# Seven half products for the gate and value products of two token groups, with a new order of the last third

## The chip, the cores and the metric

The kernel runs on one core of one Trainium2 chip. The metric is the device time of the whole program in microseconds, as the median of its runs. A core has a matrix engine (TensorE, PE in the profile), three engines for elementwise work (VectorE or DVE, ScalarE or ACT, GpSimd or POOL), and queues that start transfers (SyncE's above all, SP). Each engine works through its own list of instructions in order; semaphores hold an instruction until what it reads is written and what it overwrites is read. Matrix products end up in eight PSUM banks of 128 x 512 numbers (float32).

## The reference

Linear attention with exponential features over 8 batches, 8 heads and 576 tokens, then a feed-forward network over all 4608 tokens. Cut to what matters:

```python
def phi(x):                                   # 64 -> 128 -> 256 features
    proj = np.einsum('bhsd,df->bhsf', x, w_phi)
    proj = proj - np.max(np.abs(proj), axis=-1, keepdims=True)
    return np.concatenate([np.exp(proj), np.exp(-proj)], axis=-1)
q_p, k_p = (phi(q), phi(k))
kv = np.einsum('bhsf,bhsd->bhfd', k_p, v)
z = np.sum(k_p, axis=2)
num = np.einsum('bhsf,bhfd->bhsd', q_p, kv)
den = np.einsum('bhsf,bhf->bhs', q_p, z)[..., None] + 1e-06
x = (num / den).transpose(0, 2, 1, 3).reshape(4608, 512)
gate = np.maximum(x @ w_gate, 0.0)            # 512 -> 1536
val = x @ w_val                               # 512 -> 1536
out = gate * val @ w_out                      # 1536 -> 512
```

## The kernel before

**Groups.** The feed-forward network takes its tokens in nine groups of 512. Groups 0 to 7 are the first 512 tokens of each batch; group 8, the mixed group, holds the last 64 tokens of all eight batches. A group's x lies transposed in SBUF (`xTs`, four slots, for groups 0 to 7; `xTm` for the mixed group): 128 partitions, four blocks (`dc`) of 128 of the 512 columns. It gets there block by block: POOL normalises 128 tokens (`nx`, L947, into `xu`), and a transposing transfer from SP's queue (`xt`, L979) puts them into `xTs` or `xTm`.

**First product.** The 1536 columns of the gate and of the value weights (`wg`, `wv`) go in twelve chunks of 128. For each chunk `ffn_in` (L1081) issues four matmuls of 128 x 512 for the value product (`fv`) and four for the gate (`fg`), each into a bank. ACT (`va`, L1096) or DVE (`vb`, L1099) copies the value bank to SBUF (`val`), and DVE forms relu(gate) * value from the gate's bank and that copy into `h` (`ga`, L1102): 128 columns by 512 tokens in bf16. Of group 7 the `h` lies in two tiles of the ring `kp`, of the others in `h2` (16 slots, shown as `h`).

**Second product.** For groups 1 to 8 it is computed by seven half-sized products in place of eight. Per group, 24 half sums of `h` (four kinds for each of six pairs of chunks, 128 x 256 each; `half_sum`, L1223) are made on POOL (word `ps`) or on DVE (word `ds`; the 24 of the last part of groups 7 and 8), and differences of the weights `wo` once on POOL (`tw`, L1203). A half product (`fw`, L1247) is twelve matmuls of 128 x 256, six for each half of a bank. Copies and adds out of the banks (`ys`, `y2` on ACT, L1272 and L1275; `yw`, `yz`, `y1`, `y3`, `y4` on DVE, L1278) put the outputs together, and transfers (`ow` L1300 and others) write them out.

**Order.** A long string, `ORDER`, lists some 2,200 words such as `ga.7.4:1`: the name of a step, its arguments, the bank behind the colon, the ring slot behind the `@`. The program calls `do_<name>` for each word in turn, and each engine gets its instructions in that order. Nothing is moved afterwards. So the string alone sets what an engine does next, and an instruction that waits holds up everything behind it on its engine.

Of the kernel before, what the change touches and what calls it, by code (L numbers as in the profile page):

```python
# [16 lines left out]
ms.0 lf lm.0.0 ms.4@vr0 ms.6 id lk.0.2 lk.0.0 wq ms.3@vr1 if ms.5 zz.15:7 kf.0:0 ms.9 kf.1:1 zz.6:7  # L17
wd kh.0:0@kT0 sl k3.1.0:23 ke.0.1.0.0:2@kp0 w1:4 kg.1:1 kx.0.1.1:3@mk0 kx.0.1.0:2 wa:4 zz.2:7
k3.1.1:56 ke.0.1.3.0:6 lm.0.1 kx.0.1.2:5 zz.3:7 k0.2:0 lq.0.1 ke.0.1.3.1:6 k1.2:0@kT1 ke.0.1.0.1:2
zz.3:7 k0.0:1 ke.0.1.2.1:5 ke.0.1.1.1:3 k3.2.1:42 ke.0.1.2.0:5 kx.0.1.3:6 ms.2 lw.0.0 lw.0.1  # L20
k1.0:1@kT2 zz.5:7 k3.0.1:06 kk.0.1.0@ek0 k3.0.0:15 ke.0.1.1.0:3 ke.0.0.3.0:6@kp1 q0.1:3 lq.0.0
kx.0.2.3:2@mk1 kx.0.2.2:4 kk.0.1.1 ke.0.2.2.0:4@kp2 kx.0.0.0:1@mk2 kx.0.0.2:0 lv.0.1 ke.0.2.2.1:4
ke.0.0.1.1:5 kx.0.0.3:6 q1.1:3@qT0 ke.0.0.1.0:5 ke.0.0.3.1:6 lv.0.0 zz.6:7 q0.0:4 kx.0.0.1:5 wl.0.1
zz.4:7 k3.2.0:36 lv.0.2 ke.0.2.3.0:2 ke.0.0.2.1:0 ke.0.0.0.1:1 q1.0:4@qT1 ke.0.2.3.1:2 kx.0.2.1:6
zz.1:7 qb.1.1:5 zz.3:7 qb.0.1:4 kx.0.2.0:3 ke.0.0.0.0:1 zz.2:7 qb.0.0:2 qx.0.0.1:4 ke.0.0.2.0:0
zz.1:7 qb.1.0:1 qx.0.1.1:5 zz.7:7 qy.0.1:0 kp.0.0.0:2 ke.0.2.0.0:3 lk.1.3 kk.0.2.1@ek1 kp.0.0.1:2
kk.0.2.0 ke.0.2.1.1:6 vo.1@vs0 qx.0.1.0:1 qe.0.0.1.0:4@qp0 ke.0.2.0.1:3 qe.0.0.1.1:4 lq.1.2
qe.0.1.0.0:1@qp1 qe.0.1.0.1:1 vs.0.1.0 qz.0.1:0@my0 zz.4:7 qb.0.3:0 qx.0.0.0:2 zz.2:7 qy.0.0:3
vd.0.0.0:2@vs1 qz.0.0:3@my1 vs.0.1.1 qe.0.1.1.1:5 vp.0:2 qu.0.1@mz0 ke.0.2.1.0:6 qe.0.1.1.0:5 wl.0.0
vz.0:2 qb.0.2:4 zz.2:7 qb.1.3:3 zz.2:7 qb.1.2:1 vd.0.0.1:2 qu.0.0@mz1 vz.1:2 qe.0.1.3.0:3@qp2  # L30
vo.2@vs2 qw.0.0@cq0 qx.0.0.3:0 qx.0.0.2:4 qe.0.0.0.0:2 vs.0.2.1 zz.7:7 kv.0.0:6 qx.0.1.3:3 lw.1.1
vs.0.2.0 kc.0.0:6@kv0 kt.1.1@kT3 qe.0.0.0.1:2 kv.0.2:5 kv.0.1:6 qe.0.0.2.1:4@qp3 lm.1.1 kc.0.2:5
wl.1.1 kc.0.1:6 nu.0.0.0:2 nt.0.0.0:2@t0 zz.1:7 nu.0.0.2:5 qw.0.1 qx.0.1.2:1 qe.0.0.2.0:4
qe.0.1.3.1:3 nu.0.0.1:6 nv.0.0.0:2@u0 zz.2:7 nu.0.1.2:4 lv.1.2 nu.0.1.0:2 qe.0.1.2.1:1 nt.0.0.1:6@t1
lm.1.0 nt.0.0.2:5@t2 qy.0.2:3 nv.0.0.1:6 qe.0.0.3.0:0 nv.0.0.2:5 nt.0.1.0:2@t3 zz.2:7 nu.0.1.1:6
qy.0.3:5 nr.0.0@r0 qe.0.1.2.0:1 qz.0.2:3@my2 nv.0.1.0:2@u1 qz.0.3:5@my0 qu.0.2@mz2 zz.5:7
kr.1.1:3125 qe.0.0.3.1:0 nt.0.1.2:4@t0 nt.0.1.1:6@t1 qw.0.2 wl.1.0 nu.0.2.2:0 nx.0.0@xu0 nv.0.1.2:4
xp.0.0:7 nv.0.1.1:6 nt.0.2.2:0@t2 ke.1.1.3.1:5@kp3 nr.0.1@r1 nu.0.2.1:4 xa.0.0:7 nt.0.2.1:4@t3
nu.0.2.0:6 ke.1.1.0.1:3 nt.0.2.0:6@t0 qu.0.3@mz1 ke.1.1.0.0:3 pv.1.0:7 nv.0.2.1:4@u2 nv.0.2.2:0
nv.0.2.0:6 nu.0.3.1:4 qw.0.3 ke.1.1.1.0:1 nx.0.1@xu1 kx.1.1.0:3@mk3 xp.0.1:0 pa.1.0:7@val0  # L40
kx.1.1.3:5 pv.0.0:6 nr.0.2@r2 xa.0.1:0 nt.0.3.1:4@t1 nu.0.3.0:3 kx.1.1.1:1 nt.0.3.0:3@t3
ke.1.1.3.0:5 nu.0.3.2:7 kx.1.1.2:2 pa.0.0:6@val1 nt.0.3.2:7@t2 pv.1.1:0 nx.0.2@xu2 lw.1.0
nv.0.3.0:3@u0 xp.0.2:5 ke.1.1.1.1:1 pv.0.1:6 nv.0.3.2:7 pa.1.1:0@val2 pg.1.0:1 qt.1.1@qT2 ku.1@kT2
kk.1.1.0@ek2 ke.1.1.2.1:2 nv.0.3.1:4 pa.0.1:6@val3 lm.2.0 kt.1.0 nr.0.3@r0 nx.0.3@xu3 kk.1.1.1
qc.1.1:3076 ke.1.1.2.0:2 wl.0.2 pg.1.1:4 xa.0.2:5 pv.0.2:2 vo.1.1@vs3 qx.1.1.0:3 wl.1.2 pb.1.0:1
qe.1.1.1.0:0@qp4 qe.1.1.3.1:6@qp1 qe.1.1.0.0:3@qp0 qe.1.1.1.1:0 qx.1.1.2:7 pa.0.2:2@val0 xp.0.3:5
# [227 lines left out]
def kernel(  # L274
# [102 lines left out]
    def xT(g):  # L377
        return xT_mix if g == B else xT_all[:, g % 4]
# [985 lines left out]
```

## Time and profile before

| | |
|---|---|
| device time, median of 3 runs | 367.89 us (367.78 to 368.07) |
| span of the profiled execution | 365.2 us |
| TensorE (PE) busy | 356.6 us, 98% |
| DVE busy | 308.1 us, 84% |
| POOL busy | 275.8 us, 76% |
| ACT busy | 228.8 us, 63% |

The profile is of one execution; its own time is known by the span, first to last instruction, and the device time of the runs is 2.65 to 2.7 us longer. Busy shares are averages over stages with different limits. The page's forty slices show how the load moves (each digit is the busy share of 9.1 us in tenths):

```profile
PE   8999999999999999999999999999999999999993
DVE  5999999989999998989988989899676945448872
POOL 8765988999999999968997589946975793016600
```

TensorE is full from the second slice to the last but one. DVE and POOL are nearly full for the first two thirds and freer in the last third, where attention has ended and only the feed-forward network is left.

### The profile page before, as it was taken

To read this page: it belongs to the slowest core of one execution; us is meant where nothing else is said; L and a number is where in the kernel's file an instruction comes from. 1 tells how busy PE (TensorE), PEld (TensorE's weight loads), DVE (VectorE), ACT (ScalarE), POOL (GpSimd) and SP (SyncE) were. 2 spreads that over 40 slices of the span, in tenths; PEclk is the share of its full clock that TensorE was granted. 3 is DMA by queue.
4 is the path that set the end of the run, shared out by engine and by line. 5 is a ranking of instruction groups with operands and counts; after the bars stand their busy time and mean duration, and the time that the engine had idled before them with its cause. 6 is when DMAs were issued, how large, how long until landed. Compare 5 with 4: busy or idle time off the path is not lost.

```text
span 365.2 us, 10031 instructions
## 1 busy us (share of the span) xinstructions
PE 356.6 (98%) x3900; PEld 224.4 (61%) x3900; DVE 308.1 (84%) x723; ACT 228.8 (63%) x550; POOL 275.8 (76%) x337
## 2 busy tenths in 40 slices
PE   8999999999999999999999999999999999999993
PEld 6579865445575647755676456755457765545682
DVE  5999999989999998989988989899676945448872
ACT  4999996986698768695975278748854221121200
POOL 8765988999999999968997589946975793016600
PEclk9999999999999999999999999999999999999998
DMA  8999999983746893298219660397000320203016
GB/s 128 254 205 206 176 196 143 181 132 53 131 96 131 103 156 71 58 149 109 61 63 126 130 130 0 61 177 137 0 16 2 131 45 0 72 3 115 2 33 197
DMA packets 90768, 38.14 MB, mean 104 GB/s; under 512 B 64226, under 2 KB 86370, under 8 KB 90722
## 3 DMA queue, kind: packets, MB, share of 16 engines
q0 software_dynamic: 33504, 15.03, 32.5%
q1 hardware_dynamic: 56754, 21.83, 27.7%
q10 hardware_dynamic: 464, 0.66, 0.8%
q8 instruction: 30, 0.49, 0.6%
q14 instruction: 16, 0.13, 0.1%
HBM read 37.81 MB, written 9.44 MB: 129 GB/s over the span
## 4 chain that ended last, share of the span: by engine, by line
PE 81%; DVE 9%; POOL 4%; issue 2%; DMA 1%; ACT 1%; SPq 0%; DVEq 0%; POOLq 0%
PE bank L1081 42%; PE bank L1247 18%; PE bank L781 4%; PE bank L1110 4%; PE bank L904 3%; PE bank L1142 2%; PE bank L841 2%; PE bank L579 2%; POOL vs L1223 2%; DVE t L925 1%; DVE h L1102 1%; DVE u L935 1%; DMA w64f<-in_w_phi_dram 1%; ACT kp L675 1%; PE bank L442 1%
## 5 line engine op out<-in xcount | busy, mean ns | idle before, releaser
L675 ACT ACTIVATE kp<-bank 128x384 bf16<-128x384 f32 x192 | 84.1, 513 | 12.8 <-PE bank L579 6.0
L1081 PE MATMUL bank<-xTs,wv 128*128 128x512 bf16 x352 | 87.3, 379 | 0.0
L1096 ACT CAST val<-bank 128x512 bf16<-128x512 f32 x81 | 47.4, 592 | 62.8 <-PE bank L1081 55.7
L1081 PE MATMUL bank<-xTs,wg 128*128 128x512 bf16 x352 | 86.4, 379 | 0.0
L1102 DVE SCALAR_TENSOR_TENSOR h<-bank,val 128x512 bf16<-128x512 f32 x88 | 59.0, 681 | 22.1 <-PE bank L1081 15.0
L856 ACT ACTIVATE qp<-bank 128x512 bf16<-128x512 f32 x128 | 69.8, 619 | 5.3 <-PE bank L841 2.6
L1081 PEld LDWEIGHTS <-wg 128*128 128x128 bf16 x400 | 37.2, 98 | 41.0 <-issue 2.2
L1081 PEld LDWEIGHTS <-wv 128*128 128x128 bf16 x400 | 37.1, 98 | 38.0 <-DMA xTs<-xu 0.4
L732 POOL TENSOR_TENSOR vs<-vn,ek 128x780 bf16<-128x780 f32 (+2 forms) x40 | 53.9, 1364 | 1.2 <-ACT ek L692 0.7
L947 POOL TENSOR_TENSOR xu<-u,r 128x512 bf16<-128x512 f32 x36 | 37.3, 1044 | 16.8 <-DVE r L943 16.6
L683 DVE TENSOR_REDUCE mk<-bank 128x3 f32<-128x384 f32 x96 | 49.1, 542 | 1.0 <-ACT kp L675 0.9
L1247 PEld LDWEIGHTS <-h 128*128 128x128 bf16 x420 | 39.9, 98 | 9.5 <-issue 2.4
L1223 POOL TENSOR_TENSOR vs<-h 128x256 bf16<-128x256 bf16 x42 | 28.0, 670 | 21.4 <-DVE h L1102 14.4
L864 DVE TRANSPOSE_TENSOR_REDUCE maxq<-bank 128x16 f32<-128x512 f32 x56 | 37.1, 691 | 0.4 <-PE bank L841 0.2
L935 DVE TENSOR_TENSOR u<-bank,t 128x195 f32<-128x195 f32 (+1 forms) x108 | 32.7, 327 | 0.7
L925 DVE TENSOR_TENSOR t<-bank,cq 128x195 f32<-128x195 f32 (+1 forms) x96 | 29.4, 325 | 2.0 <-PE bank L904 1.7
L1247 PE MATMUL bank<-wo,h 128*128 128x256 bf16 x252 | 31.0, 273 | 0.0
L904 PEld LDWEIGHTS <-qp 128*128 128x128 bf16 x512 | 23.2, 98 | 10.8 <-issue 1.2
L1223 POOL TENSOR_TENSOR vs<-vs,h 128x256 bf16<-128x256 bf16 x42 | 27.9, 673 | 1.0 <-PE bank L1247 0.2
L904 PE MATMUL bank<-kv,qp 128*128 128x65 bf16 x512 | 26.1, 193 | 0.4 <-DVE u L935 0.2
L1223 POOL TENSOR_TENSOR h<-h 128x256 bf16<-128x256 bf16 x36 | 23.7, 670 | 0.3
L1223 POOL TENSOR_TENSOR h<-h,vs 128x256 bf16<-128x256 bf16 x36 | 23.7, 671 | 0.0
(134 smaller groups left out, 577.3 us busy)
## 6 DMA issues: line engine op xcount, KB each, us to landing
vn<-in_v_dram SPq DMA_DIRECT2D x24, 256.0 KB, 5.5
out_dram<-xTs SPq DMA_DIRECT2D x17, 256.0 KB, 2.4
kn<-in_k_dram POOLq DMA_DIRECT2D x7, 512.0 KB, 8.6
qn<-in_q_dram POOLq DMA_DIRECT2D x7, 512.0 KB, 8.0
out_dram<-obp SPq DMA_DIRECT2D x14, 256.0 KB, 2.4
wv<-in_moe_w_val_dram POOLq DMA_DIRECT2D x3, 512.0 KB, 8.9
wg<-in_moe_w_gate_dram POOLq DMA_DIRECT2D x3, 512.0 KB, 9.3
wo<-in_moe_w_out_dram POOLq DMA_DIRECT2D x3, 512.0 KB, 8.2
```

The costliest lines, as they stand in the source:

```text
L675: nc.scalar.activation(kp_of(3 * b + j)[:, i, s].rearrange("p n f -> p (n f)"), bank[bk[0]][:, 0 : 3 * F], AF.Exp, scale=(1.0, -1.0)[s],)
L683: nc.vector.tensor_reduce(mk_of(3 * b + j)[:, :, i], bank[bk[0]][:, 0 : 3 * F].rearrange("p (n f) -> p n f", f=F), axis=AX.X, op=ALU.max, ...
L732: nc.gpsimd.tensor_tensor(vs_of(3 * b + j)[:, s, 0:n].rearrange("p n i e -> p (n i) e")[:, :, 0:e], src[:, lo:hi].rearrange("p h i e -> p ...
L856: nc.scalar.activation(qp_of(4 * b + i)[:, s, 4 * hq : 4 * hq + 4].rearrange("p h m -> p (h m)"), bank[bk[0]], AF.Exp, scale=(1.0, -1.0)[s],)
L864: nc.vector.tensor_reduce((maxq0[:, i] if b == 0 else maxq)[:, :, i, 4 * hq : 4 * hq + 4].rearrange("p t h -> p h t"), bank[bk[0]].rearran ...
L904: nc.tensor.matmul(bank[bk[0]][:, E * n : E * (n + 1)], lhsT=qp_of(4 * b + i)[:, s, h, :], rhs=kv_of(b)[:, h, s, 0:E],)
L947: eng.tensor_tensor(xu_of(n).rearrange("p (h d) -> p h d", d=D), u_of(n)[:, :, 0:D], r_of(n).to_broadcast([P, H, D]), op=ALU.mult,)
L1081: nc.tensor.matmul(bank[bk[0]], lhsT=w[:, dc, P * f : P * f + P], rhs=xT(g)[:, dc, :], start=(dc == 0), stop=(dc == NDC - 1),)
L1096: nc.scalar.copy(val_of(NFC * g + f), bank[bk[0]])
L1102: nc.vector.scalar_tensor_tensor(h2_of(g, f), bank[bk[0]], 0.0, val_of(NFC * g + f), op0=ALU.max, op1=ALU.mult)
L1223: eng.tensor_tensor(sum_of(g, n, j), a, b, op=op)
L1247: nc.tensor.matmul(bank[bk[0]][:, col : col + HN], lhsT=x[:, P * u : P * (u + 1)], rhs=w, start=(n in (1, 5, 6) and u == us[0] and j == 0) ...
```

## The change

The first product of two groups, 8 and 7, is now computed together, with seven half products in place of eight. As a block product, the rows are the tokens of group 8 (x1, x2: the two halves of the 512 columns of x) and of group 7 (x3, x4), and the columns are the gate and the value weights, each in an upper and a lower half. With S1 = x3 + x4, S2 = S1 - x1, S3 = x1 - x3, S4 = x2 - S2 for the tokens and T1 = wv_lo - wg_lo, T2 = wv_hi - T1, T3 = wv_hi - wv_lo, T4 = wg_hi - T2 for the weights, seven products of two matmuls each are made per chunk: P1 = x1 wg_lo, P2 = x2 wg_hi, P3 = S4 wv_hi, P4 = x4 T4, P5 = S1 T1, P6 = S2 T2, P7 = S3 T3. The gate of group 8 is P1 + P2; its value P1 + P6 + P3 + P5; the value of group 7 is P1 + P6 + P7 + P5, its gate P1 + P6 + P7 + P4.

- The word `fi.p.f.n` is product n of chunk f (two matmuls; p = 0 is the only pair). It takes the place of `fv` and `fg` of groups 7 and 8.
- P1 is needed twice more: ACT copies its bank to another bank (`ia`), TensorE adds P6 there, and ACT copies that bank to a third (`ib`). P5 is copied to SBUF by ACT (`iq`, into a float32 tile of the ring `u`).
- DVE forms the two values as bank plus that copy (`iv`, two for each chunk). They replace the copies `va` and `vb` of groups 7 and 8. The gate of group 7 is made in the bank that its value was read from, so P4 follows `iv`.
- POOL makes the token sums (`xs`, eight operations of 128 x 512, L1169) and the weight sums (`wt`, 24 of 128 x 512, L1142). T3 overwrites the lower half of `wv`.
- The 24 half sums that DVE made (`ds`) are now made on POOL (`ps`). One copy of the keys' product moves from ACT to DVE.
- The `h` of group 7 lies in one `kp` tile, one `qp` tile and two slots of `h2`.
- `ORDER` is new for its last quarter (from about 241 us in the trace on); ahead of that only banks and ring slots have other numbers.

```diff
     def h2_of(g, f):
         i = NFC * g + f
-        if g == B - 1:
-            t = kp_of(("h", g, f // 6)).rearrange("p i s n f -> p (i s n f)")
-            return t[:, SF * (f % 6) : SF * (f % 6 + 1)]
+        if g == B - 1 and f < 6:
+            t = kp_of(("h", g)).rearrange("p i s n f -> p (i s n f)")
+            return t[:, SF * f : SF * (f + 1)]
+        if g == B - 1 and f < 10:
+            t = qp_of(("h", g)).rearrange("p s h m -> p (s h m)")
+            return t[:, SF * (f - 6) : SF * (f - 5)]
...
+    PAIRS = ((8, 7),)
...
+    def weight_sum(eng, n, dc, third):
+        cols = slice(SF * third, SF * (third + 1))
+        at = lambda t, d: t[:, d, cols]
+        a, b = {
+            1: lambda: (at(wv_sb, dc), at(wg_sb, dc)),
+            2: lambda: (at(wv_sb, 2 + dc), at(w_sum(1), dc)),
+            3: lambda: (at(wv_sb, 2 + dc), at(wv_sb, dc)),
+            4: lambda: (at(wg_sb, 2 + dc), at(w_sum(2), dc)),
+        }[n]()
+        eng.tensor_tensor(at(w_sum(n), dc), a, b, op=ALU.subtract)
+
+    def do_wt(bk, n, dc, third):
+        weight_sum(nc.gpsimd, n, dc, third)
...
+    def token_sum(eng, p, n, dc):
+        a, b, op = {
+            1: lambda: (x_part(p, 3), x_part(p, 4), ALU.add),
+            2: lambda: (x_sum(p, 1), x_part(p, 1), ALU.subtract),
+            3: lambda: (x_part(p, 1), x_part(p, 3), ALU.subtract),
+            4: lambda: (x_part(p, 2), x_sum(p, 2), ALU.subtract),
+        }[n]()
+        eng.tensor_tensor(x_sum(p, n)[:, dc], a[:, dc], b[:, dc], op=op)
+
+    def do_xs(bk, p, n, dc):
+        token_sum(nc.gpsimd, p, n, dc)
+
+    def do_fi(bk, p, f, n):
...
+        for dc in range(2):
+            nc.tensor.matmul(
+                bank[bk[0]],
+                lhsT=w[:, dc, P * f : P * f + P],
+                rhs=x[:, dc, :],
+                start=(n in (1, 5) and dc == 0),
+                stop=(dc == 1),
+                skip_group_check=(n not in (1, 5)),
+            )
+
+    def do_ia(bk, p, f):
+        nc.scalar.copy(bank[bk[1]], bank[bk[0]])
+
+    def do_ib(bk, p, f):
+        nc.scalar.copy(bank[bk[1]], bank[bk[0]])
+
+    def do_iq(bk, p, f):
+        nc.scalar.copy(q_evicted(p, f), bank[bk[0]])
...
+    def do_iv(bk, p, f, u):
+        nc.vector.tensor_tensor(
+            val_of(NFC * PAIRS[p][u] + f), bank[bk[0]], q_evicted(p, f), op=ALU.add
+        )
```

Two lines of the new `ORDER`, from its middle:

```python
iv.0.3.0:2@val2 iv.0.3.1:0@val1 fi.0.0.4:6 fi.0.6.1:5 fi.0.3.2:7 fi.0.6.5:2 wt.2.0.2 ia.0.6:51
fi.0.9.5:0 iq.0.8:6@u1 fi.0.6.4:1 iv.0.4.0:4@val1 iv.0.7.1:3@val0 wt.2.1.2 ps.6.4.4 wt.3.0.2
```

The instructions of POOL in the stretch in which group 7's x is finished. Rows give the line, the operation, out<-in and the shape; `xu` is a normalised block, `qT` and `qr` hold token sums, `vn`, `kp` and `wv` weight sums, and `vs` and `h` half sums. Before:

```order
L947 TENSOR_TENSOR xu_135<-u_127,r_131 128x512
L1223 TENSOR_TENSOR h_152<-h_152,vs_98 128x256 x2
L1223 TENSOR_TENSOR vs_97<-h_152 128x256
L1223 TENSOR_TENSOR h_152<-h_152,vs_98 128x256
L1223 TENSOR_TENSOR vs_100<-vs_97,h_152 128x256
L1223 TENSOR_TENSOR vs_97<-h_152 128x256
```

After the same normalisation in the new program:

```order
L960 TENSOR_TENSOR xu_133<-u_127,r_131 128x512
L1337 TENSOR_TENSOR vs_98<-h_152 128x256
L1169 TENSOR_TENSOR qT_108<-xTs 128x512 x2
L1169 TENSOR_TENSOR qT_107<-qT_108,xTm 128x512
L1337 TENSOR_TENSOR h_152<-h_152 128x256
L1337 TENSOR_TENSOR vs_97<-vs_98,h_152 128x256
L1337 TENSOR_TENSOR h_152<-h_152 128x256
L1169 TENSOR_TENSOR qT_107<-qT_108,xTm 128x512
```

Token sums, which read the transposed x in `xTs` and `xTm`, stand between the half sums of group 6; the weight sums follow behind them, among half sums.

The end of POOL's list, with the half sums of groups 8 (`h`, `vs`) and 7 (`kp`, `qp`, `vs`), before:

```order
L1223 TENSOR_TENSOR vs_101<-kp_82,kp_81 128x256 x2
L1223 TENSOR_TENSOR vs_99<-vs_101,kp_82 128x256
L1223 TENSOR_TENSOR vs_100<-vs_97,h_152 128x256 x3
L1223 TENSOR_TENSOR vs_101<-kp_82,kp_81 128x256 x3
L1223 TENSOR_TENSOR vs_99<-vs_101,kp_82 128x256 x5
```

And of the new program:

```order
L1337 TENSOR_TENSOR vs_101<-kp_83,qp_112 128x256
L1337 TENSOR_TENSOR vs_98<-vs_101,kp_83 128x256 x3
L1337 TENSOR_TENSOR h_152<-h_152,vs_99 128x256 x2
L1337 TENSOR_TENSOR vs_98<-vs_101,kp_83 128x256 x2
L1337 TENSOR_TENSOR h_152<-h_152,vs_99 128x256
L1337 TENSOR_TENSOR kp_83<-kp_83 128x256
L1337 TENSOR_TENSOR h_152<-h_152,vs_99 128x256 x3
L1337 TENSOR_TENSOR kp_83<-kp_83 128x256 x3
L1337 TENSOR_TENSOR h_152<-h_152,vs_98 128x256
L1337 TENSOR_TENSOR qp_112<-qp_112,vs_98 128x256 x4
L1337 TENSOR_TENSOR h_152<-h_152,vs_98 128x256
```

The sums that overwrite `h`, `kp` and `qp` (third and fourth kind) now close POOL's list. Before they stood near the end of DVE's, between the adds of the output:

```order
L1223 TENSOR_TENSOR kp_81<-kp_81,vs_99 128x256
L1223 TENSOR_TENSOR kp_82<-kp_82 128x256
L1278 TENSOR_TENSOR xTs<-bank_65,xTs 128x2x256
L1223 TENSOR_TENSOR kp_81<-kp_81,vs_99 128x256 x2
L1223 TENSOR_TENSOR h_152<-h_152,vs_100 128x256
L1278 TENSOR_TENSOR obp<-bank_66,obp 128x2x256
L1223 TENSOR_TENSOR h_152<-h_152,vs_100 128x256
L1278 TENSOR_TENSOR obp<-bank_64,obp 128x2x256
```

The same place of DVE's list in the new program, where only the adds are left behind the last product with relu:

```order
L1118 SCALAR_TENSOR_TENSOR qp_112<-bank_67,val_141 128x512
L1392 TENSOR_TENSOR xTm<-bank_68,obp 128x2x256
L1392 TENSOR_TENSOR obp<-bank_68,obp 128x2x256 x2
L1392 TENSOR_TENSOR obp<-bank_64,obp 128x2x256
L1392 TENSOR_TENSOR xTs<-bank_69,xTs 128x2x256
L1392 TENSOR_TENSOR xTm<-bank_64,xTm 128x2x256
L1392 TENSOR_TENSOR xTs<-bank_69,xTs 128x2x256
```

More of the change, by code (lines that the diff above doesn't have):

```diff
@@ L23 @@
[L23 to L46, printed above, removed]
```

533 lines of the change are left out of this document (304 added, 229 removed).

## The prediction

> **What bounds the kernel now.** Read the page's busy times first, then the chain of waits, then the windows of the last 85 us (columns: stretch, length, then busy time and count of PE, PEld, DVE, ACT, POOL, the granted clock, DMA share, GB/s).
>
> ```profile
> span 365.2 us, 10031 instructions
> PE 356.6 (98%) x3900; PEld 224.4 (61%) x3900; DVE 308.1 (84%) x723; ACT 228.8 (63%) x550; POOL 275.8 (76%) x337
> PE 81%; DVE 9%; POOL 4%; issue 2%; DMA 1%; ACT 1%; SPq 0%; DVEq 0%; POOLq 0%
> 280.00:300.00 20.00, 20.00 (x253) 14.29 (x251) 13.17 (x44) 5.17 (x11) 17.66 (x27) 1.00 0.28 80
> 300.00:320.00 20.00, 20.00 (x112) 10.75 (x110) 10.31 (x16) 3.01 (x6) 4.68 (x7) 1.00 0.11 33
> 320.00:340.00 20.00, 20.00 (x100) 9.70 (x99) 13.12 (x23) 4.26 (x8) 8.61 (x13) 1.00 0.15 54
> 340.00:350.00 10.00, 10.00 (x84) 8.03 (x82) 8.30 (x16) 2.48 (x5) 5.29 (x8) 1.00 0.01 2
> ```
>
> TensorE is busy in every microsecond of this stretch at full clock, and the chain runs on it for 81% of the span. POOL is the freest engine there: 13.3 us of 40 between 300 and 340. The timeline says how TensorE is paid.
>
> ```profile
> 302.71 1.03 PE L1081 MATMUL bank<-xTm,wg 128*128 128x512 bf16 x4
> 303.57 1.03 PE L1081 MATMUL bank<-xTm,wv 128*128 128x512 bf16 x4
> 342.03 1.47 PE L1247 MATMUL bank<-wo,h 128*128 128x256 bf16 x12
> 357.75 1.47 PE L1247 MATMUL bank<-wo,kp 128*128 128x256 bf16 x12
> 359.26 0.42 DVE L1278 TENSOR_TENSOR xTs<-bank,xTs 128x256 f32<-128x256 f32 x1 [0.23 <-PE bank L1247]
> ```
>
> Four matmuls of 128x512 start 0.86 us after the four before them: 0.2155 each. The thirteen groups of twelve half-wide matmuls from 342.03 end with the last at 357.75 + 1.31 = 359.06 (1.31 is (357.75 - 342.03)/12): 0.109 per matmul, no gap. The last add starts 0.20 later, and the final output's transfer follows it. From TensorE's end to the span's end are 365.24 - 359.06 = 6.18 us, and the median of the runs, 367.89, lies 2.65 above the span. So **time = TensorE's end + 8.83**, if what follows the last matmul stays; the after's order ends in the same way (last half product, one add, one output transfer).
>
> **The change, part by part.** *Removed from TensorE.* Twelve chunks x two products x eight matmuls become twelve x seven x two: 192 - 168 = 24 fewer, and 24 x 0.2155 = 5.17 us. With no new stall TensorE ends at 353.89.
>
> *Added to POOL.* Eight token sums and 24 weight sums (512 wide, two bf16 inputs), and 24 half sums of groups 7 and 8 that DVE made.
>
> ```profile
> 240.98 2.04 POOL L947 TENSOR_TENSOR xu<-u,r 128x512 bf16<-128x512 f32 x2 [3.42 <-DVE r L943]
> 282.26 0.67 POOL L1223 TENSOR_TENSOR vs<-h 128x256 bf16<-128x256 bf16 x1
> 282.89 0.67 POOL L1223 TENSOR_TENSOR vs<-vs,h 128x256 bf16<-128x256 bf16 x1
> 284.15 0.67 POOL L1223 TENSOR_TENSOR vs<-h 128x256 bf16<-128x256 bf16 x1
> 284.89 1.30 POOL L1223 TENSOR_TENSOR vs<-vs,h 128x256 bf16<-128x256 bf16 x2
> L947 POOL TENSOR_TENSOR xu<-u,r 128x512 bf16<-128x512 f32 x36 | 37.3, 1044 | 16.8 <-DVE r L943 16.6
> L732 POOL TENSOR_TENSOR vs<-vn,ek 128x780 bf16<-128x780 f32 x24 | 35.5, 1497 | 0.5 <-ACT ek L692 0.4
> L732 POOL TENSOR_TENSOR vs<-vn,ek 128x520 bf16<-128x520 f32 x12 | 12.6, 1061 | 0.3 <-ACT ek L692 0.3
> L760 POOL TENSOR_TENSOR vr<-vm,ek 64x520 bf16<-64x520 f32 x14 | 14.8, 1059 | 1.3 <-ACT ek L692 0.7
> L1203 POOL TENSOR_TENSOR kp<-wo 128x768 bf16<-128x768 bf16 x4 | 6.6, 1647 | 0.0
> ```
>
> Starts lie some 0.04 us before the end of the one ahead, so an operation holds POOL for its duration less 0.04: a half sum 0.63 (282.26 to 282.89). A 512-wide sum of two bf16 inputs is not in the trace. By the rows of 256 (0.63) and 768 (1.60) it is the midpoint, 1.11; by the 512-wide normalisation it is 1.00. I take **1.11**, since those rows are of the same form. The normalisations at 240.98 stand at the same place of both orders, and nothing ahead of them changes but names of banks and buffers. From there to its end POOL has, in the new order, 94 half sums, 32 of the new sums, 10 normalisations, 4 value products of 780, 2 of 520 and 2 of the 64-row kind: 94 x 0.628 + 32 x 1.11 + 10 x 1.00 + 4 x 1.45 + 2 x 1.01 + 2 x 1.02 = 114.4 us (before: 114.4 - 24 x 0.628 - 35.5 = 63.8). **With no wait at all POOL ends at 355.4**, later than the 353.89 of TensorE. POOL takes the bound over.
>
> *The end.* The last sum is the sixth fourth-kind sum of group 7. Behind it TensorE has one half-wide matmul of the first half and the six of the second, 0.11 + 0.66: end at 356.2.
>
> *POOL's waits.* Each goes straight to the end.
>
> ```profile
> 242.05 3.42 SPq L979 DMA_TRANSPOSE xTs<-xu  x1
> 287.96 1.22 SPq L979 DMA_TRANSPOSE xTm<-xu  x1
> xTm<-xu SPq DMA_TRANSPOSE x4, 3.2
> 324.16 0.67 POOL L1223 TENSOR_TENSOR vs<-kp,kp 128x256 bf16<-128x256 bf16 x1 [15.48 <-DVE kp L1102]
> ```
>
> Three of the eight sums that make group 8's inputs (second kind, and what follows) wait for the transposed last block of the mixed group; its normalisation ends at about 285.7 by my sum over POOL's order, and 3.2 us to landing (row of issues) make 288.9, where POOL stands ready at 288.5: 0.4 us. Where a sum reads what the one ahead wrote, starts lie 0.74 apart (284.15 to 284.89), 0.11 more; about eight such pairs stand in the new order: 0.9. Sum 1.3. Below, it could be 0; above, the row at 324.16 shows POOL waiting 15.48 us for group 7's h in one go, so the upper end is open; what speaks for a small one is that POOL, at its new load, comes later to every sum of groups 6 to 8 than before, so that the h it reads has had longer to be ready. I take **1.3: TensorE ends at 357.5 to 357.6, 1.5 us earlier than before, time 366.4**.
>
> *Removed from DVE.* 24 half sums and seven value copies go; 24 adds of a bank to a buffer come, and one copy of the keys' products.
>
> ```profile
> L1223 DVE TENSOR_TENSOR kp<-kp,vs 128x256 bf16<-128x256 bf16 x6 | 1.6, 281 | 0.0
> 344.23 3.37 POOL L1223 TENSOR_TENSOR vs<-vs,kp 128x256 bf16<-128x256 bf16 x5
> 344.34 0.75 DVE L1223 TENSOR_TENSOR kp<-kp 128x256 bf16<-128x256 bf16 x1
> 353.32 0.28 DVE L1223 TENSOR_TENSOR kp<-kp,vs 128x256 bf16<-128x256 bf16 x1
> L1278 DVE TENSOR_TENSOR obp<-bank,obp 128x512 f32<-128x512 f32 x21 | 14.2, 681 | 4.3 <-PE bank L1247 4.3
> L1102 DVE SCALAR_TENSOR_TENSOR h<-bank,val 128x512 bf16<-128x512 f32 x88 | 59.0, 681 | 22.1 <-PE bank L1081 15.0 <-ACT val L1096 5.1 <-PE bank L1247 1.1
> ```
>
> The new adds read a bank and a buffer, as the last two rows do (0.681): 24 x 0.68 = 16.3 us. The half sums cost DVE 0.28 each alone and 0.75 beside POOL's, 6.7 to 18 us in all. So DVE's load rises by at most some 10 us, in 70 (280 to 350) in which the windows leave it 70 - 13.17 - 10.31 - 13.12 - 8.30 = 25 idle: nothing on the path by its load alone. In before's tail POOL made five sums at 3.37/5 = 0.675 while DVE summed from buffers, and at 0.63 where DVE did not: I use 0.628 for the tail's 22, since no DVE sum with two buffer inputs is left there. The Trainium skill, "SBUF — State Buffer", section "Who interferes with whom", states that a DVE instruction with two SBUF inputs contends with a GpSimd instruction that reads SBUF, and that one with at most one SBUF input doesn't; the 0.675 and 0.75 agree with it. Without that rule the 22 sums would take 22 x 0.047 = 1.0 us more and the time would be 367.4.
>
> *Evictions.* 24 copies of values (17 on ACT, 7 on DVE) go; 36 copies on ACT come, 24 of them from bank to bank.
>
> ```profile
> L703 ACT ACTIVATE bank<-mk 128x12 f32<-128x12 f32 x2 | 0.4, 180 | 0.0
> L1096 ACT CAST val<-bank 128x512 bf16<-128x512 f32 x25 | 14.3, 587 | 41.0 <-PE bank L1081 36.6 <-DVE h L1102 4.2
> ```
>
> No 512-wide copy into a bank is in the trace; the value copies (0.587) are its nearest row, the 12-wide write (0.18) bounds it below, and the adds of 0.681 above. I take 0.59. A chunk then needs 3 x 0.59 = 1.8 us of ACT and 4 x 0.68 = 2.7 us of DVE (two adds, two products with relu) beside 14 x 0.2155 = 3.02 us of TensorE: each fits. But a product that adds to a bank now waits for the copy into it, and the order leaves such waits no slack: at six places, walking the new order with these prices gives -0.2 to +0.1 us. Up to 1.2 us of TensorE's stalls there are free, since POOL reaches the tail's sums at 341.6 and group 7's last h is ready at 340.4 without stalls.
>
> **The rivals.**
>
> *(a) The forecast*, POOL the bound at the end: from waits 0 to 2.0, TensorE's end 356.2 to 358.2, time 365.0 to 367.0. For it: 114.4 us in 118.
>
> *(b) POOL is cheaper, TensorE stays the bound.* With 1.00 per 512-wide sum POOL saves 32 x 0.11 = 3.5 and ends at 351.9 + waits; then eviction stalls of 0 to 1.5 on 353.89 set the end: 362.7 to 364.3. Against it: the bf16 rows.
>
> *(c) All is given back*, by 1.5 us more of POOL's waits for h, as TensorE's stalls behind the bank copies exceed the free 1.2 us: end 359.1, time 367.9. Work that is saved only moves the wait; this is also how it looks if the matmuls saved come back as stalls.
>
> *(d) Slower, by the token sums' wait for the transposes.* If the transposed blocks of group 7 and the mixed group come later, as with the one at 242.05 that took 3.42 us to issue where the one at 287.96 took 1.22, POOL stands still at its fullest place, all weight sums slip, and with them the matmuls that read them: 1.2 for the wait on group 7's block and 1.5 for the mixed group's, 2.7 in all, end 360.3, time 369.1. It decides as soon as POOL's waits from 240.98 on sum to over 1.3 + 1.5 + 0.7 = 3.5 us. For it: even before, POOL stands idle for 2.3 us of 280 to 300, where it is fullest.
>
> That the change doesn't remove the matmuls is excluded: the program has 7729 TensorE instructions where 7777 stood.
>
> **How the numbers follow.** (a) 0.50, (b) 0.12, (c) 0.18, (d) 0.20. Faster by over 0.2% (0.74 us, about what a measurement of this kernel can tell from no change) means under 367.15: (a) and (b), 0.62. Within 0.2%: (c), 0.18. Slower: (d), 0.20. The likeliest is (a): **366.4**. The range leaves out the lower two thirds of (b) and the tail of (d) beyond 369.6, some 0.15: from 363.9 to 369.6; the own range of (a) is 365.0 to 367.0.
>
> **What would show it.** TensorE: 3876 matmul records, fewer by 24; its last matmul ends at about 357.6, with gaps of together 3 to 4 us after 300, most of them ended by POOL in the last 15 us. POOL: busy over 19 of each 20 us from 280 on; token and weight sums of 1.15 (1.11 + 0.04); the last half sum ends at about 356.7. ACT: bank copies of 0.59. Wrong would be: 512-wide sums near 1.04 (then b); gaps of TensorE ended by ACT or DVE that sum to over 3 us (c); a gap of POOL of over 1 us ahead of a token sum, ended by a DMA (d).

## The result, and the profile after

| | before | after |
|---|---|---|
| device time, median | 367.98 us (367.78 to 368.26, 4 runs) | 362.22 us (361.98 to 362.58, 4 runs) |
| ratio, 95% interval | | 0.9847 (0.9833 to 0.9861) |
| span of the profiled execution | 365.2 us | 360.8 us |
| last matmul, nominal end | 359.06 | 357.06 |
| last matmul to the span's end | 6.2 | 3.7 |

The change makes the kernel 5.8 us faster, below the predicted range. First the page of the changed kernel (span, busy times, chain of waits), then its windows (same columns as before).

```profile
span 360.8 us, 10067 instructions
PE 354.0 (98%) x3876; PEld 222.5 (62%) x3876; DVE 309.8 (86%) x717; ACT 238.1 (66%) x568; POOL 325.0 (90%) x393
PE 68%; POOL 19%; DVE 8%; issue 2%; ACT 2%; POOLq 0%; DVEq 0%
280.00:300.00 20.00, 20.00 (x125) 12.06 (x124) 8.60 (x17) 7.60 (x14) 20.00 (x26) 1.00 0.30 73
300.00:320.00 20.00, 20.00 (x105) 9.95 (x103) 16.30 (x26) 9.21 (x17) 20.00 (x21) 1.00 0.01 2
320.00:340.00 20.00, 20.00 (x122) 11.83 (x121) 15.68 (x26) 7.97 (x15) 20.00 (x30) 1.00 0.15 53
340.00:350.00 10.00, 9.87 (x89) 8.52 (x88) 4.05 (x6) 0.59 (x1) 10.00 (x17) 1.00 0.01 2
```

POOL is busy in all of each window from 280 on, and TensorE has no gap before 340. The chain, which ran on POOL for 4% before, runs on it for 19%. The next rows are groups of POOL, ACT and DVE (line, shapes, count, busy, mean ns) and the first and the last instruction of POOL's stretch from the common place on.

```profile
L1142 POOL TENSOR_TENSOR vn<-wv,wg 128x512 bf16<-128x512 bf16 x6 | 6.9, 1154 | 0.0
L1169 POOL TENSOR_TENSOR qT<-qT,xTm 128x512 bf16<-128x512 bf16 x2 | 2.3, 1170 | 0.0
L1204 ACT COPY bank<-bank 128x512 f32<-128x512 f32 x12 | 6.9, 572 | 10.7 <-PE bank L1194 7.7 <-DVE h L1118 1.1 <-DVE val L1216 1.0
L1216 DVE TENSOR_TENSOR val<-bank,u 128x512 bf16<-128x512 f32 x24 | 15.7, 684 | 4.4 <-PE bank L1194 3.1 <-ACT bank L1207 1.3
241.57 2.04 POOL L960 TENSOR_TENSOR xu<-u,r 128x512 bf16<-128x512 f32 x2 [3.42 <-DVE r L956]
355.55 0.67 POOL L1337 TENSOR_TENSOR h<-h,vs 128x256 bf16<-128x256 bf16 x1
```

From 241.57 to the end of its last sum (356.22) are 114.65 us; the sum of POOL's operations without any wait was 114.4. Between those two rows POOL's timeline names no idle time before any instruction. The 512-wide sums last 1.15 us (their starts lie 1.11 apart), the bank copies 0.57, the adds 0.68. Now the end: the last rows of TensorE, DVE and the two queues, and TensorE's waits from 300 on (us, times, longest).

```profile
351.89 1.56 PE L1361 MATMUL bank<-kp,kp 128*128 128x256 bf16 x11 [0.19 <-POOL kp L1337]
354.24 0.60 PE L1361 MATMUL bank<-qp,qp 128*128 128x256 bf16 x4 [0.78 <-DVE xTs L1392]
356.84 0.38 PE L1361 MATMUL bank<-wo,h 128*128 128x256 bf16 x2
357.05 0.35 SPq L1414 DMA_DIRECT2D out_dram<-xTs  x1
357.26 0.42 DVE L1392 TENSOR_TENSOR xTs<-bank,xTs 128x256 f32<-128x256 f32 x1 [0.23 <-PE bank L1361]
357.71 0.35 ACTq L1437 DMA_DIRECT2D out_dram<-xTs  x1
PE bank L1361 <- DVE xTs L1392: 0.8, 1, 0.8
PE bank L1361 <- POOL kp L1337: 0.2, 1, 0.2
```

The one long wait of TensorE, 0.8 us for an add of DVE, goes back to POOL as well: that add waited 1.17 us for a product whose half sums POOL finished at 352.46. The last matmul ends at 356.84 + 2 x 0.109 = 357.06, and the last transfer's issue at 358.06; the span ends 2.7 us later. In the kernel before the last issue is that of ACT's queue:

```profile
359.64 0.94 ACTq L1323 DMA_DIRECT2D out_dram<-xTs  x1
```

It ends at 360.58, and the span 4.7 us later. What the transfers do there is in the windows of the end (the last two columns are the share of the transfer engines and GB/s), three of before and three of after, with the time from a transfer's issue to its landing from 340 on (shortest, median, longest).

```profile
354.00:358.00 4.00, 4.00 (x39) 3.59 (x38) 2.64 (x7) 0.00 (x0) 0.00 (x0) 1.00 0.73 198
358.00:362.00 4.00, 1.23 (x12) 0.85 (x9) 1.46 (x3) 0.00 (x0) 0.00 (x0) 1.00 0.93 239
362.00:365.00 3.00, 0.00 (x0) 0.00 (x0) 0.00 (x0) 0.00 (x0) 0.00 (x0) 0.67 0.35 117
DMA to landing us min/median/max: 2.3/3.1/4.9
```

```profile
350.00:354.00 4.00, 3.25 (x27) 2.22 (x26) 1.20 (x2) 0.58 (x1) 4.00 (x7) 1.00 0.89 225
354.00:358.00 4.00, 2.96 (x24) 2.08 (x23) 2.47 (x6) 0.00 (x0) 2.22 (x4) 1.00 0.94 271
358.00:361.00 3.00, 0.00 (x0) 0.00 (x0) 0.00 (x0) 0.00 (x0) 0.00 (x0) 1.00 0.37 125
DMA to landing us min/median/max: 2.2/2.6/3.7
```

Both kernels write the outputs of groups 7 and 8 in a block of some 9 us in which the transfer engines are 0.9 busy. Before, this block begins at about 354 and goes on for some 4 us behind the last matmul. After, it begins at 350, and TensorE's last matmul comes near its end. The first transfers of the block are issued here, before and after:

```profile
353.43 1.20 SPq L1304 DMA_DIRECT2D out_dram<-obp  x2
349.02 2.49 SPq L1418 DMA_DIRECT2D out_dram<-obp  x4
```

The block starts 4.4 us earlier, while the last matmul ends only 2.0 us earlier.

### The profile page after: what moved, and what is told of

Its sections match the earlier page's. It is cut to its first block, busy times and chain, and to the rows that moved or that the text cites. A ratio compares the mean times of both kernels' runs of the same rounds, so it can differ in the third digit from the quotient of the medians.

```text
span 360.8 us, 10067 instructions
## 1 busy us (share of the span) xinstructions
PE 354.0 (98%) x3876; PEld 222.5 (62%) x3876; DVE 309.8 (86%) x717; ACT 238.1 (66%) x568; POOL 325.0 (90%) x393
## 4 chain that ended last, share of the span: by engine, by line
PE 68%; POOL 19%; DVE 8%; issue 2%; ACT 2%; POOLq 0%; DVEq 0%
PE bank L1097 32%; PE bank L1361 13%; POOL vs L1337 6%; PE bank L794 5%; POOL h L1337 4%; PE bank L1224 4%; PE bank L917 3%; POOL kp L1142 3%; PE bank L854 2%; PE bank L592 2%; PE bank L1256 2%; PE bank L455 2%; POOL wv L1142 2%; POOL qT L1169 2%; ACT kp L688 2%
## 5 line engine op out<-in xcount | busy, mean ns | idle before, releaser
L1097 PE MATMUL bank<-xTs,wv 128*128 128x512 bf16 x304 | 75.6, 379 | 0.0
L1097 PE MATMUL bank<-xTs,wg 128*128 128x512 bf16 x304 | 75.5, 379 | 0.0
L1118 DVE SCALAR_TENSOR_TENSOR h<-bank,val 128x512 bf16<-128x512 f32 x90 | 60.4, 679 | 10.7 <-ACT val L1112 6.2
L1112 ACT CAST val<-bank 128x512 bf16<-128x512 f32 x64 | 37.8, 594 | 34.0 <-PE bank L1097 26.1
L1361 PEld LDWEIGHTS <-h 128*128 128x128 bf16 x432 | 41.0, 98 | 10.7 <-issue 2.9
L1097 PEld LDWEIGHTS <-wg 128*128 128x128 bf16 x304 | 27.8, 98 | 30.0 <-issue 2.0
L1097 PEld LDWEIGHTS <-wv 128*128 128x128 bf16 x304 | 27.6, 98 | 27.0 <-issue 0.4
L1361 PE MATMUL bank<-wo,h 128*128 128x256 bf16 x260 | 32.5, 273 | 0.0
L1337 POOL TENSOR_TENSOR h<-h,vs 128x256 bf16<-128x256 bf16 x44 | 28.9, 669 | 0.0
L1337 POOL TENSOR_TENSOR h<-h 128x256 bf16<-128x256 bf16 x42 | 27.7, 669 | 0.2
```

The lines of the kernel that those rows point to most:

```text
L1097: nc.tensor.matmul(bank[bk[0]], lhsT=w[:, dc, P * f : P * f + P], rhs=xT(g)[:, dc, :], start=(dc == 0), stop=(dc == NDC - 1),)
L1112: nc.scalar.copy(val_of(NFC * g + f), bank[bk[0]])
L1118: nc.vector.scalar_tensor_tensor(h2_of(g, f), bank[bk[0]], 0.0, val_of(NFC * g + f), op0=ALU.max, op1=ALU.mult)
L1337: eng.tensor_tensor(sum_of(g, n, j), a, b, op=op)
L1361: nc.tensor.matmul(bank[bk[0]][:, col : col + HN], lhsT=x[:, P * u : P * (u + 1)], rhs=w, start=(n in (1, 5, 6) and u == us[0] and j == 0) ...
```

## The experiments

Theories: **transfers** (in the kernel before, the backlog of output transfers, those issued and not yet carried out, and not the last matmul sets the end) against **last matmul** (what lies behind the last matmul is a constant, as the prediction had it), and whether POOL is the bound at the end.

**The output transfers cut out, before and after.** All but the last two transfers of groups 7 and 8 are left out, and in the changed kernel one of group 5 that stood among them:

```diff
-... yz.7:2 ow.8.2
-y1.7.1:4 oq.7.0.0 ow.8.3 ds.7.4.5 fw.7.5.0:5 fw.7.4:2 y4.8:1 y1.7.0:5 ds.7.4.0 oq.7.1.1 y3.7:2
-fw.7.3.1:4 ov.0 fw.7.3.0:5 y4.7.1:4 ov.1 oq.7.1.0 y4.7.0:5 ow.7.0.1 oz.7.1
+... yz.7:2
+y1.7.1:4 ds.7.4.5 fw.7.5.0:5 fw.7.4:2 y4.8:1 y1.7.0:5 ds.7.4.0 y3.7:2
+fw.7.3.1:4 fw.7.3.0:5 y4.7.1:4 y4.7.0:5 ow.7.0.1 oz.7.1
```

> The kernel before without the output transfers of groups 7 and 8, but for the last two (one on each queue); their rows are not written. TRANSFERS theory: the last 9 us of before are bound by the backlog of output transfers (DMA share 0.97 and 0.88 between 358 and 362), and the last two land 4.3 and 4.6 us after their issue because of it. Without the others they land in about 2.4, the last matmul stays at 359.1, and the time falls by about 2.0 us, to 366.0. LAST MATMUL theory (the prediction's sum): what lies behind the last matmul is a constant 8.83 us, time 368.0.

> The changed kernel with the same cut (all output transfers of groups 7 and 8 but the last two left out, and one late transfer of group 5). TRANSFERS theory: its last two transfers land 2.2 and 2.6 us after issue already, so at most 0.4 us are to be had: 361.8 to 362.2, and the distance between the two cut kernels is about 4.0 us where it is 5.8 between the whole ones. LAST MATMUL theory: 362.2, distance 5.8.

Measured beside the kernel before at 367.36 us (366.36 to 368.19, 13 runs): the cut kernel before 364.79 (ratio 0.9930, 0.9908 to 0.9951), the cut changed kernel 362.05 (0.9857, 0.9835 to 0.9878). The first row is the last matmul group of the cut kernel before, then the issue of its last transfer and the landing times:

```profile
358.45 1.47 PE L1246 MATMUL bank<-wo,kp 128*128 128x256 bf16 x12
360.41 0.33 SPq L1299 DMA_DIRECT2D out_dram<-xTs  x1
DMA to landing us min/median/max: 1.7/1.7/1.7
```

Its last matmul ends at 359.76, no earlier than before's 359.06, and yet the time falls by 2.6 us: its two transfers land 1.7 us after their issue, where the same two took 4.3 and 4.6 in the kernel before. The changed kernel gains 0.2 us from the same cut, less than its own medians differ (362.22 to 362.69). The distance between the two, 5.8 us uncut (5.1 by the runs of before that stand beside these), is 2.7 cut (4.0 was expected). So 2.4 to 3.1 us of the difference between the kernels are the backlog that the changed one no longer has to wait for. For the kernel before, the transfers theory holds.

The two cut kernels also show what lies behind the last matmul when no backlog does: their spans end 3.44 us (363.2 - 359.76) and 3.57 us (360.8 - 357.23) behind it. In the changed kernel it is 3.74, in the kernel before 6.18.

**The backlog thinned, nothing else.** In the kernel before, the first quarter of the mixed group's output goes out when it is ready:

```diff
-... ds.7.3.0 y2.8:0
+... ds.7.3.0 y2.8:0 o8
...
+    def do_o8(bk):
+        for t in range(2):
+            for bb in range(2):
+                r0 = S * (2 * t + bb) + SF
+                nc.sync.dma_start(
+                    out=out[r0 : r0 + SM, 0:HN],
+                    in_=ow_pair(B, 0)[SM * bb : SM * (bb + 1), t, 0:HN],
+                )
```

with `do_ov` writing the other 256 columns alone.

> The kernel before, whole, with one change: the first quarter of the mixed group's output (256 KB, ready at 344.1) is issued then, in place of with its other columns at 357 to 359. No matmul, sum or add moves. TRANSFERS theory: of 2.1 MB in the backlog 256 KB go, at about 235 GB/s 1.1 us; last matmul unmoved, time about 1.0 us below the kernel before in the same call. LAST MATMUL theory: no change.

365.60 us against 367.81 for the kernel before beside it (0.9941, 0.9929 to 0.9954): 2.2 us, twice what was expected, with every matmul, sum and add as before. Windows of its end:

```profile
358.00:360.00 2.00, 1.46 (x14) 1.07 (x11) 1.50 (x3) 0.00 (x0) 0.00 (x0) 1.00 0.83 246
360.00:362.00 2.00, 0.00 (x0) 0.00 (x0) 0.00 (x0) 0.00 (x0) 0.00 (x0) 1.00 0.92 275
362.00:364.00 2.00, 0.00 (x0) 0.00 (x0) 0.00 (x0) 0.00 (x0) 0.00 (x0) 1.00 0.01 4
```

The transfers end at 362 where they went on into the window from 362 to 365. Its last two transfers land in 2.8 and 2.7 us, and its last matmul ends at 359.30. 256 KB at 240 GB/s explain 1.1 us; between the two profiled executions the gain is 1.4 us (spans 365.2 and 363.8), and why the medians differ by 2.2 was not tried. The shape of the rest changed too (rows of 1 KB in place of 2 KB on ACT's queue), and the rate between 360 and 362 is 275 GB/s where before's from 358 to 362 is 239.

**The matmuls alone, taken out and put back.**

```diff
-        for dc in range(NDC):
+        n = NDC - 1 if g >= 7 and w is wg_sb else NDC
+        for dc in range(n):
```

> The kernel before with 24 matmuls fewer and nothing else: the gate products of groups 7 and 8 leave out their last 128 of 512 columns of x. If the matmuls that go are what the change gains (24 x 0.2155 = 5.17 us, no stall of TensorE in the place), the time is 362.8. If the gain of the change is mostly that of its new order, this gains clearly less than 4 us (over 364).

```diff
-        for dc in range(2):
+        dcs = (0, 1, 1) if n in (2, 7) else (0, 1)
+        for i, dc in enumerate(dcs):
```

> The changed kernel with 24 matmuls added back (the second and the seventh half product add their second block of columns twice, so the output is another). TensorE's stalls for POOL behind 345 us (2.0 us) go, since POOL comes less late: its last matmul moves from 357.1 to about 360.3. TRANSFERS theory: the output transfers of the tail start 4.5 to 5.2 us later and the time goes with them: 366.7 to 367.4. LAST MATMUL theory: 362.2 + 3.2 = 365.4.

The kernel before with 24 matmuls fewer takes 362.55 (0.9862, 0.9836 to 0.9889), 4.8 us less than the 367.36 beside it; with nothing but TensorE's work gone, the transfers of the tail start earlier and the whole backlog moves. The first transfers of its block, its last matmuls and a window behind them:

```profile
348.93 1.20 SPq L1305 DMA_DIRECT2D out_dram<-obp  x2
353.25 1.47 PE L1248 MATMUL bank<-wo,kp 128*128 128x256 bf16 x12
356.00:358.00 2.00, 0.00 (x0) 0.00 (x0) 0.00 (x0) 0.00 (x0) 0.00 (x0) 1.00 0.91 250
```

The last matmul ends at 354.56, and the span 6.5 us later (361.1), with the backlog still there. The changed kernel issues the first of these transfers at the same time (349.02), ends its matmuls 2.5 us later, at 357.06, and takes the same time within 0.4 us. **The stalls that POOL makes in the last 12 us thus fall into the time that the output transfers need anyway.**

The changed kernel with 24 matmuls more takes 366.99 (0.9986, 0.9976 to 0.9996), some 4.3 to 4.8 us above the changed kernel. This run doesn't tell the theories apart as it was meant to: its last matmul came at 361.2 and not at 360.3, because POOL, which never waited in the changed kernel, now waits for DVE's products:

```profile
329.42 0.67 POOL L1338 TENSOR_TENSOR vs<-h 128x256 bf16<-128x256 bf16 x1 [2.67 <-DVE h L1118]
336.10 0.67 POOL L1338 TENSOR_TENSOR vs<-kp,qp 128x256 bf16<-128x256 bf16 x1 [0.99 <-DVE qp L1118]
339.66 0.67 POOL L1338 TENSOR_TENSOR vs<-h 128x256 bf16<-128x256 bf16 x1 [0.38 <-DVE h L1118]
```

These waits sum to 2.67 + 0.99 + 0.38 = 4.0 us, for 5.2 us of work added to TensorE. So POOL was late by only about 1 us: TensorE's work and POOL's are nearly balanced.

**POOL made longer.** Two weight sums are made twice in a row.

```diff
-wt.1.1.2 ... wt.1.0.2
+wt.1.1.2 wt.1.1.2 ... wt.1.0.2 wt.1.0.2
```

> The changed kernel with two of its weight sums made twice in a row on POOL (2 x 1.11 us more, same result), some 40 us ahead of the end. If POOL is busy without a gap to the last sum, and TensorE waits for it at the end, both ends come 2.2 us later; since the transfers leave 0.2 us of cover (the kernel without them gained that), the time is 364.2. If POOL isn't the bound, under 363.

364.61 us (0.9921, 0.9907 to 0.9935, beside 367.51). The changed kernel took 362.22, 362.69 and 362.48 in its three sets of runs, so this is 1.9 to 2.4 us more for 2.2 us of POOL. The last sum starts at 357.69 in place of 355.55. The last two transfers land in 1.7 and 2.0 us, about as fast as without a backlog, so it is not the transfers that set this end. When POOL gets longer it is the bound at the end, as the prediction had it; what a shorter POOL gains is another question.

**POOL made shorter.** The last six half sums on DVE (`ps.7.4.0` to `ps.7.4.5` become `ds`), then with one, then with two output transfers issued early:

```diff
-ow.5.1 fw.7.6:6 ... fw.8.3:1 ps.7.4.4 ps.7.4.3 ps.7.4.2 y4.8:1
-ov.0 ps.7.4.0 ps.7.4.1 ov.1 ps.7.4.5 fw.7.7:6 yz.7:6
+ow.5.1 fw.7.6:6 ... fw.8.3:1 ds.7.4.4 ds.7.4.3 ds.7.4.2 y4.8:1
+ov.0 ds.7.4.0 ds.7.4.1 ov.1 ds.7.4.5 fw.7.7:6 yz.7:6
```

> The changed kernel with the last six half sums of group 7 (fourth kind) on DVE in place of POOL, at the same places of the order. DVE is busy for under half of the last 17 us. POOL ends about 3.7 us earlier, TensorE's waits for it (1.2 of them ahead of the last half product) mostly go, and its last matmul moves from 357.1 to about 355.7. TRANSFERS theory: the output transfers start when they did (350.1) and need their 9 us, so nearly nothing is gained: 361.8 to 362.2. LAST MATMUL theory: the time falls with it, 360.8.

> The kernel with the six sums on DVE, and with one 256 KB output transfer of group 5 issued behind group 5's others, some 20 us ahead, where it stood among the last transfers. TRANSFERS theory: 2.1 MB are left where 2.4 MB were in the last 9 us, at about 250 GB/s 1.0 us less, until TensorE's end (355.7 + 3.5) sets it: 361.0. LAST MATMUL theory: as without it, 360.8.

> As the one before, and the first quarter of the mixed group's output (256 KB, ready at 341) is issued on its own as soon as it is ready, in place of with the rest at 352 to 355. TRANSFERS theory: another 1.0 us of transfers leaves the tail, TensorE's end is the bound (355.7 + 3.5 + 1.78): 360.4 to 360.9, and this and the one before show how far transfers were the bound.

Beside 367.51: 363.48 (0.9891, 0.9873 to 0.9909), 362.89 (0.9873, 0.9855 to 0.9890) and 362.83 (0.9879, 0.9860 to 0.9899). Neither theory's number came, since the last matmul did not come earlier (356.9 to 357.5): POOL ended at 351.9 to 352.4, but DVE's sums stood behind it. POOL's last sums of the first of the three kernels, DVE's first one, and TensorE's wait that followed:

```profile
349.31 0.69 POOL L1337 TENSOR_TENSOR h<-h,vs 128x256 bf16<-128x256 bf16 x1
349.93 1.95 POOL L1337 TENSOR_TENSOR kp<-kp 128x256 bf16<-128x256 bf16 x3
349.68 2.34 DVE L1337 TENSOR_TENSOR h<-h,vs 128x256 bf16<-128x256 bf16 x1 [0.52 <-PE bank L1361]
354.29 0.60 PE L1361 MATMUL bank<-qp,qp 128*128 128x256 bf16 x4 [1.41 <-DVE xTs L1392]
```

One sum of 128x256 took 2.34 us on DVE; it ended when POOL's last did, at 351.9 to 352.0. In the other two kernels the same sum took 2.40 and 2.38. The adds that free TensorE's banks were queued behind it. These kernels leave open whether POOL's tail is worth anything. They show that a sum on DVE can be dear in a tail where POOL doesn't pause; what all 24 would cost there was not tried.

**The tail in another order.** With the two early transfers kept, group 7's third sums go ahead of group 8's fourth, the seventh half product of group 7 ahead of the third of group 8, and three sums to DVE behind the adds (or none). The cut shows the last lines:

```diff
...
-ow.5.1 fw.7.6:6 fw.7.2:7 y2.7:7 yw.7:6 oq.7.0.0 ps.7.3.5 fw.8.3:1 ps.7.4.4 ps.7.4.3 ps.7.4.2 y4.8:1
-ov.0 ps.7.4.0 ps.7.4.1 ov.1 ps.7.4.5 fw.7.7:6 yz.7:6 fw.7.4:6 y1.7.0:0 y1.7.1:2 oq.7.1.1 y3.7:6
+fw.7.6:6 fw.7.2:7 y2.7:7 yw.7:6 oq.7.0.0 fw.7.7:6 fw.8.3:1 ps.7.4.4 ps.7.4.3 ps.7.4.2 yz.7:6 y1.7.0:0 y1.7.1:2
+oq.7.1.1 ds.7.4.0 ds.7.4.1 ds.7.4.5 y4.8:1
+ov.0 ov.1 fw.7.4:6 y3.7:6
```

> The changed kernel itself once more, for the comparison with the kernels of this call: 362.2 if the chip is like that of the first runs, with the kernel before 5.1 to 5.8 us above it.

> The changed kernel with its tail put in another order: group 7's third sums ahead of group 8's fourth, seventh product of group 7 ahead of the third of group 8 (so that the add that frees its bank lies beside matmuls), three of the last sums on DVE behind the adds, and the two output transfers issued early as before. POOL ends at about 353.7 in place of 356.2, the last matmul at 355.9 in place of 357.1, and the early transfers leave no backlog: 361.0. If DVE's three sums stand behind POOL's as they did with six (2.3 us for one), nothing is gained: 362.2.

> As the one before, with all sums on POOL. POOL is the bound at the end, as in the changed kernel: its last sum at about 356.2, last matmul 357.0, time 362.0 to 362.3, whatever the order of the tail and of the transfers.

Beside 367.81: the changed kernel 362.69 (0.9867, 0.9850 to 0.9884), three sums on DVE (a_v3) 362.93 (0.9873, 0.9859 to 0.9886), all on POOL (a_v4) 362.29 (0.9853, 0.9840 to 0.9867). The intervals of the three overlap, so the new order and the early transfers gain nothing that is clear. With three on DVE the last matmul came at 355.6 and nothing was gained, as the last transfer of the output was issued at 357.8 all the same: on ACT's queue it stood behind four transfers, and those behind an add that DVE made only after its sums. That add ahead of the sums (a_v5, beside 367.63):

```diff
-oq.7.1.1 ds.7.4.0 ds.7.4.1 ds.7.4.5 y4.8:1
+y4.8:1 oq.7.1.1 ds.7.4.0 ds.7.4.1 ds.7.4.5
```

> The changed kernel with the tail of a_v3, and DVE's last add of the mixed group ahead of its three half sums, so that the mixed group's last transfers are issued from 353.9 on. POOL ends at about 354, the last matmul at 356.0, the last transfer is issued at 356.7 in place of 357.7. If POOL's tail and the last matmul are the bound of the changed kernel, the time is 0.8 to 1.0 us below it: 361.4 to 361.8. If the transfers are, within 0.3 of it.

> The changed kernel for the comparison with a_v5 on the same chip: 362.2 to 362.7.

361.94 us (361.61 to 362.01; 0.9840, 0.9825 to 0.9854) against 362.48 (362.14 to 362.90; 0.9857, 0.9841 to 0.9874) for the changed kernel beside it. The last rows of TensorE and of ACT's queue of a_v5, then the last of TensorE of the changed kernel beside it:

```profile
355.60 0.38 PE L1362 MATMUL bank<-wo,h 128*128 128x256 bf16 x2
356.65 0.56 ACTq L1447 DMA_DIRECT2D out_dram<-xTs  x1
356.20 0.38 PE L1361 MATMUL bank<-wo,h 128*128 128x256 bf16 x2
```

The runs of the two don't overlap, but their intervals against the kernel before do. The last matmul ends 0.6 us earlier than in that profile of the changed kernel, the last transfer is issued 0.4 earlier (there at 357.08), and the time is 0.5 less. This lies between the two expectations, and a_v5 also has the early transfers and the new order, with which a_v4, all sums on POOL, lay 0.4 us below the changed kernel beside it. So it isn't shown that POOL's tail still holds the time back; if it does, these runs put it at about half a microsecond. This is the fastest version of the study, by little.

## Why the prediction missed

The forecast was 366.4; the time was 362.22. The 4.2 us between them are, by the two profiled executions:

| step of the prediction | predicted | measured | time |
|---|---|---|---|
| last matmul after POOL's normalisations at 240.98 (after: 241.57) | 116.6 | 115.5 | -1.1 |
| that common place itself | 240.98 | 241.57 | +0.6 |
| last matmul to the span's end | 6.18 | 3.74 | -2.4 |
| time above the span | 2.65 | 1.78 | -0.9 |
| profiled execution against the median (362.58 and 362.22) | 0 | -0.4 | -0.4 |

1. **The step that failed is "time = TensorE's end + 8.83, if what follows the last matmul stays".** It did not stay. The prediction read the chain of waits, which follows the last add back to TensorE, and took the 6.18 us behind the last matmul for a fixed latency. The windows show the transfer engines 0.93 busy there; the cut kernel and the thinned backlog show that the transfers were the bound (2.6 and 2.2 us to be had without moving a matmul earlier). Only 3.4 to 3.6 of the 6.18 us stand without a backlog, by the two cut kernels. With 3.5 us there and 1.78 from span to time, the prediction's own last matmul (357.57) would have given about 362.9. Output transfers begin when the first products of the tail are done, and TensorE's saving arrives there (4.4 us) before POOL's stalls do. So most of the 5.17 us of matmuls passes through, as the kernel with only these 24 matmuls removed shows (4.8 us), and the stalls that follow lie beside the transfers. In the changed kernel the two ends, that of POOL's sums and that of the transfers, then come at nearly the same time: taking the transfers away gains 0.2 us, and the best kernel with a shorter tail of POOL lies 0.5 below it.
2. The same sum mixed two executions. The time of a run is about 1.78 us above its span (1.72 to 1.85) in every run for which both are listed (362.58 and 360.8, for one). By that, the profiled execution of before took 367.0 us, 1.0 less than the median of 367.98 (one listed run of before with a span of 365.2 took 367.03); taking the 2.65 for an offset carried this scatter into the forecast.
3. **POOL as the bound at the end was right**, and so was its price: 114.4 us without waits were 114.65, a 512-wide sum 1.11, and two more of them cost 1.9 to 2.4 us. The waits of 1.3 us were mis-sized: POOL had none to speak of (0.25 us over 114). The 0.4 for the transposed block and the 0.9 for dependent neighbours did not appear. The 0.9 was read from one pair of rows 0.74 apart; a pair of the same form in the new program (261.05 and 261.67) lies 0.62 apart. That the last matmul came within half a microsecond of the forecast is partly luck: this error and a common place 0.6 us later point opposite ways.
4. Rival (d), the token sums behind the transposes, did not happen; the trace names no wait of POOL behind the common place. Rival (c), TensorE's stalls behind the bank copies, did not happen either: TensorE is busy for all of 280 to 340, though the walk through the order gave no slack. Copies between banks took 0.572, a little less than the 0.59 assumed.
5. Rival (b) gave a time (362.7 to 364.3) close to the measured one, by another mechanism and so by luck: POOL was not cheaper, its lateness was covered. (The stated range from 363.9 leaves out three quarters of (b), not two thirds.)
6. The prediction let POOL's sums of the tail run at 0.628 us, since no DVE sum with two buffer inputs is left there: so they did (1.91 us for three sums, starts 0.63 apart). The rule of the Trainium skill, "SBUF — State Buffer", section "Who interferes with whom", that a DVE instruction with two SBUF inputs contends with a GpSimd instruction that reads SBUF, and that one with at most one does not outside DVE's two-port modes, agrees with this and with the 2.34 us of the DVE sum beside POOL's.

The matmuls' part and the backlog's part of the gain are not two gains that add: in the kernel before the backlog was late because TensorE was, and the change moved both. What remains open is why the thinned backlog gave 2.2 us and not 1.1, and whether the 0.3 to 1.0 us between the change's gain and that of the missing matmuls, which is not clear of the noise, belongs to the new order of the tail.

## What to carry to other kernels

Ask of the end of a kernel what ends last there, the last compute or the last byte: read the transfer share and the landing times behind the last matmul before calling that stretch a constant, since the chain of waits stops at the last instruction. Where a backlog of output is the bound, work saved ahead of the first output transfer can count nearly in full, and stalls behind it may cost nothing. And never add the offset of a median to the span of one profiled execution; compare the span with the time of that same run.

## What the runs showed of the hardware

- A 128x256 half sum with two SBUF inputs takes DVE 0.28 us alone and took 2.34, 2.40 and 2.38 us in three kernels while POOL's sums ran back to back; each time it ended within 0.2 us of the last of them. POOL took 1.95 us for three sums in that stretch, where it took 1.91 in the changed kernel: there the delay fell almost wholly on DVE.
- A copy of 128x512 float32 from bank to bank takes ACT 0.572 us, one from a bank to SBUF 0.591 in the same kernel.
- A 128 KB output transfer lands 1.7 us after its issue with no other output transfers in the tail; the same two took 4.3 and 4.6 us in the backlog.
- POOL ran 144 elementwise operations in 114.65 us, 0.25 us more than their prices by start-to-start distances of the kernel before (1.11 for the 512-wide sums, a midpoint) add up to.
